# Attention with cached K and V on one core: x transposed on TensorE instead of by DMA, dummy products at the start, new order tables and load pacing

## The chip, the core and the metric

The kernel runs on one core of a Trainium2 chip. The core has a matrix engine (TensorE, in the profile PE, with its weight loads as PEld), three engines that work on rows of 128 partitions (VectorE, DVE; ScalarE, ACT; GpSimd, POOL), a queue engine that only issues transfers here (SyncE, SP), and 16 DMA engines that move data between the memory (HBM) and the on-chip memory (SBUF). TensorE writes into PSUM, which has eight banks of 128 partitions by 512 float32; the other engines read the banks and write SBUF. The metric is the time of one execution on the device in microseconds (us).

## What is computed

Two attention blocks, A and B, with the same shapes and their own inputs, written side by side into one output:

```python
B, Sq, D = 16, 64, 640
H, Sk, Dh = 32, 512, 128        # all arrays bfloat16

q = (x @ wq).reshape(B, Sq, H, Dh).transpose(0, 2, 1, 3)
scores = jnp.einsum("bhqd,bhkd->bhqk", q, k_cache) * (Dh ** -0.5)
p = softmax(scores, axis=-1)
o = jnp.einsum("bhqk,bhkd->bhqd", p, v_cache)
y = o.transpose(0, 2, 1, 3).reshape(B, Sq, H * Dh) @ wo
...
return jnp.concatenate([a, b], axis=-1)      # of blocks A and B
```

K and V of both blocks are 4 x 67 MB. All other inputs and the output are small beside them.

## The kernel before

**Tiles.** The batches are taken in pairs, so that the 64 queries of two batches fill 128 partitions; a pair and a head make a tile g. Two tiles (two heads of one pair) make a *step* m, two steps a *period* k. Sixteen heads of a pair make a group of four periods, and a pass is eight pairs with one half of the heads; there are four passes (block A heads 0 to 15, A 16 to 31, B, B), so 256 steps and 128 periods.

**One step.** K of two heads is loaded in rows and transposed by TensorE against an identity (KX, line 550: 32 products of 64 columns into two banks), copied to SBUF by VectorE (KE, 557). The scores of a tile are two products (SM, 596). VectorE takes the negated row maximum (MX, 605), ACT the exponential with the row sum (EX, 621), VectorE the reciprocal of two sums (RC2, 627), GpSimd multiplies (NM, 635). TensorE transposes the normalized P of a step, eight products into one bank (TR2, 644); the bank is copied to SBUF whole, for even steps by ACT (TA2, 656) and for odd steps by VectorE (TE2, 651). Then come the products with V (PV2, 666), one copy per period by ACT (OE4, 673), and the output projection, whose first 512 columns are done step by step (OP2, 681) and the other 128 once in a group (OX, 691). After an even pass ACT keeps the sums in `outp` (OVP and OXP, 699 and 704); after an odd one VectorE adds to them (OVF and OXF, 709 and 714) and ACT issues the store (ST, 720).

**Q.** The queries are made from x transposed (`xT_sb`, 128 rows of D by columns of queries). Sixteen heads of four pairs are needed at a time. The first of these are made in the first periods by QJ and QZ, the later ones, one per period, by QN (all line 567; five products over D); ACT copies them with the scale (QEJ, QEZ, QEN, 583). x of block A comes in by three DMA transposes (LDX, 751) of one, three and four pairs; x of block B comes later in plain rows (LDXR, 769), is transposed by TensorE (XT, 776: five products of 128 columns) and copied by ACT (XTE, 783).

**Order.** Nothing is scheduled on the chip. `build_plan` sorts each engine's list by a time in steps, which the tables `PHASES` give: for each kind of operation an offset in steps and a place within a period of `PERIOD` = 6.3. A table holds from a period on: here from 0, 16, 112 and from two before the end. Waits on semaphores follow from what each operation reads and writes. Banks: 0 sums, 1 the V products (and early Q), 2 to 5 scores (P^T uses 2 and 3, the 128 columns and x use 4), 6 and 7 K.

**Loads.** All loads are on SP's queue, in the order of a key: the step of first use less a lead (`LEAD` for K and V, `WLEAD` for weights). The planner also makes each load wait until TensorE has passed a position in its list, so that it is not issued far ahead:

```python
    for key, first, _, op in sorted(loads, key=lambda e: e[:3]):
        t_now = max(t_now, us(key))
        i = bisect.bisect_right(pe_us, min(t_now, us(first - cfg.BEFORE))) - 1
        if i >= 0:
            paced.append((op, progs["pe"][i]))
        progs["sp"].append(op)
        t_now += cfg.DMA_US[op.kind] * (op.aux[2] - op.aux[1] if op.kind == "LDX" else 1)
```

`us` turns steps into microseconds by the stretches of `STEP_US`; `t_now` starts at `START_US` and adds an assumed cost per load. So each load waits until TensorE has passed the place that stands for the earlier of two times: `t_now` (its key, or later where the loads ahead of it are assumed to take longer), and `BEFORE` steps ahead of its first use. Behind schedule, then, the second time binds. Nine K tiles (`NKB`) and five periods of V (`NVP`) fit on the chip.

## Time and profile before

| | us |
|---|---|
| median of three runs | 856.32 (855.03 to 856.79) |
| profiled execution | 857.66 |
| its span in the trace | 855.9 |
| TensorE busy | 805.9 (94%) |
| VectorE busy | 726.6 (85%) |
| ACT busy | 633.0 (74%) |
| GpSimd busy | 418.0 (49%) |
| moved by DMA | 297.13 MB, mean 347 GB/s |

How to read it: the page gives busy time by engine, then the span in 40 equal slices (each digit is the busy share in tenths; the last rows are the DMA engines' share and what they moved in GB/s). A busy share is an average over stages with different limits, so windows, waits and the timeline are read by stage. In a timeline or window line, xN is the number of instructions; what stands in brackets at the end is the engine's idle time before and what ended it. In the chain of work that ended last, each line is a start, a length and what ran or was waited for; a DMA line begins at its issue and ends with its landing. "SPq" is SP's queue itself. L numbers are lines of the kernel before.

### The profile page before, as it was taken

What the parts mean: (1) busy time and instruction counts of PE and PEld (TensorE: products, weight loads), DVE (VectorE), ACT (ScalarE), POOL (GpSimd) and SP (SyncE); (2) the same over time, 40 slices, a digit from 0 to 9 for tenths busy, and PEclk for the clock granted to TensorE, in tenths of its full rate; (3) what the DMA queues carried; (4) which work ended last, traced back from release to release, by engine and by line L of the source; (5) the groups of instructions that cost most, each with busy time, mean ns of one, the idle gap of its engine ahead of it and who ended that gap; (6) DMA issues with size and microseconds to landing.
All of it is one profiled execution on the core that took longest, in us unless ns stands there. A gap on an engine that the chain in (4) does not pass through costs nothing.

```text
span 855.9 us, 38296 instructions
## 1 busy us (share of the span) xinstructions
PE 805.9 (94%) x16953; PEld 561.8 (66%) x17084; DVE 726.6 (85%) x1184; ACT 633.0 (74%) x1450; POOL 418.0 (49%) x518
## 2 busy tenths in 40 slices
PE   5999999999999999999999899999999999999987
PEld 3566666666666766766666666666676666666665
DVE  3588888898888899898898788988888889889995
ACT  2677787787787777777777777777877867767775
POOL 0344554545544554554554445555455545446554
DMA  8999999999999999999999999999999999999993
GB/s 266 321 368 367 357 352 328 358 352 346 356 363 354 355 364 366 359 368 369 366 354 368 316 355 364 360 358 362 355 363 364 364 360 370 346 307 350 368 352 115
DMA packets 232581, 297.13 MB, mean 347 GB/s; under 512 B 14304, under 2 KB 166880, under 8 KB 232416
## 3 DMA queue, kind: packets, MB, share of 16 engines
q1 hardware_dynamic: 230112, 292.06, 100.2%
q8 instruction: 133, 2.18, 1.1%
q10 hardware_dynamic: 2304, 2.62, 0.9%
q14 instruction: 32, 0.26, 0.1%
HBM read 290.72 MB, written 2.62 MB: 343 GB/s over the span
## 4 chain that ended last, share of the span: by engine, by line
PE 81%; DMA 9%; DVE 3%; issue 3%; ACT 2%; POOL 1%; SPq 1%; POOLq 0%; ACTq 0%; DVEq 0%
PE ps L550 15%; PE ps L567 14%; PE ps L666 14%; PE ps L596 13%; PE ps L644 11%; PE ps L681 11%; DMA v_ring<-in_B_v_cache_dram 6%; PE ps L691 3%; DMA v_ring<-in_A_v_cache_dram 3%; DVE ktp_ring L557 2%; DVE negmax L605 1%; POOL pn_ring L635 1%; ACT p_ring L621 1%; DMA wq_sb<-in_A_wq_dram 1%; ACT pT_ring L656 1%
## 5 line engine op out<-in xcount | busy, mean ns | idle before, releaser
L635 POOL TENSOR_SCALAR pn_ring<-p_ring,recip 128x512 bf16<-128x512 bf16 x512 | 417.4, 846 | 429.9 <-DVE recip L627 403.2
L621 ACT ACTIVATE p_ring<-ps,negmax 128x512 bf16<-128x512 f32 x512 | 350.0, 689 | 77.5 <-DVE negmax L605 74.3
L557 DVE COPY ktp_ring<-ps 128x2048 bf16<-128x2048 bf16 x256 | 311.9, 1218 | 78.6 <-PE ps L550 78.3
L605 DVE TENSOR_REDUCE negmax<-ps 128x1 f32<-128x512 f32 x512 | 320.6, 683 | 19.7 <-PE ps L596 12.6
L550 PEld LDWEIGHTS ps<-ident,kn_ring 64*128 64x128 bf16 x8192 | 135.8, 95 | 99.2 <-issue 58.8
L550 PE MATMUL ps<-ident,kn_ring 64*128 64x64 bf16 x8192 | 167.4, 191 | 5.3 <-DVE ktp_ring L557 2.6
L673 ACT ACTIVATE oT_ring<-ps 128x512 bf16<-128x512 f32 x128 | 76.4, 597 | 123.7 <-PE ps L666 123.7
L567 PE MATMUL ps<-xT_sb,wq_sb 128*128 128x512 bf16 (+2 forms) x544 | 135.7, 376 | 26.8 <-issue 18.3
L666 PE MATMUL ps<-pT_ring,v_ring 128*128 128x64 bf16 x4096 | 142.7, 193 | 7.4 <-DMA v_ring<-in_B_v_cache_dram 4.1
L644 PEld LDWEIGHTS ps<-ident,pn_ring 128*128 128x128 bf16 x2048 | 124.9, 98 | 34.8 <-ACT p_ring L621 3.4
L644 PE MATMUL ps<-ident,pn_ring 128*128 128x128 bf16 x2048 | 137.4, 219 | 1.7 <-POOL pn_ring L635 1.2
L596 PE MATMUL ps<-ktp_ring,qc_ring 128*64 128x512 bf16 x1024 | 137.6, 387 | 1.2 <-issue 1.1
L666 PEld LDWEIGHTS ps<-pT_ring,v_ring 128*128 128x128 bf16 x4096 | 127.4, 98 | 15.9 <-DMA v_ring<-in_B_v_cache_dram 5.3
L681 PE MATMUL ps<-wo_sb,oT_ring 128*128 128x512 bf16 x497 | 132.1, 379 | 5.0 <-ACT pT_ring L656 2.5
L656 ACT ACTIVATE pT_ring<-ps 128x1024 bf16<-128x1024 bf16 x128 | 132.6, 1036 | 0.6 <-PE ps L644 0.4
L621 ACT ACTIVATION_READ_ACCUMULATOR p_ring<-ps,negmax 128x1 f32 x512 | 105.2, 206 | 0.0
L567 PEld LDWEIGHTS ps<-xT_sb,wq_sb 128*128 128x128 bf16 x660 | 54.9, 99 | 62.8 <-DMA wq_sb<-in_A_wq_dram 7.7
L651 DVE COPY pT_ring<-ps 128x1024 bf16<-128x1024 bf16 x128 | 86.3, 674 | 6.9 <-PE ps L644 6.8
L583 ACT ACTIVATE qc_ring<-ps 128x512 bf16<-128x512 f32 (+1 forms) x129 | 77.1, 597 | 14.2 <-PE ps L567 14.2
L596 PEld LDWEIGHTS ps<-ktp_ring,qc_ring 128*64 128x64 bf16 x1024 | 47.3, 109 | 37.4 <-issue 5.0
L681 PEld LDWEIGHTS ps<-wo_sb,oT_ring 128*128 128x128 bf16 x512 | 43.4, 98 | 31.8 <-ACT pT_ring L656 4.6
L627 DVE RECIPROCAL recip<-rowsum 128x2 f32<-128x2 f32 x256 | 39.9, 156 | 9.1 <-ACT p_ring L621 9.1
(16 smaller groups left out, 109.1 us busy)
## 6 DMA issues: line engine op xcount, KB each, us to landing
kn_ring<-in_A_k_cache_dram SPq DMA_DIRECT2D x128, 512.0 KB, 6.7
v_ring<-in_A_v_cache_dram SPq DMA_DIRECT2D x128, 512.0 KB, 6.6
kn_ring<-in_B_k_cache_dram SPq DMA_DIRECT2D x128, 512.0 KB, 6.4
v_ring<-in_B_v_cache_dram SPq DMA_DIRECT2D x128, 512.0 KB, 6.3
wq_sb<-in_A_wq_dram SPq DMA_DIRECT2D x8, 640.0 KB, 6.6
wo_sb<-in_A_wo_dram SPq DMA_DIRECT2D x8, 640.0 KB, 6.8
wq_sb<-in_B_wq_dram SPq DMA_DIRECT2D x8, 640.0 KB, 6.4
wo_sb<-in_B_wo_dram SPq DMA_DIRECT2D x8, 640.0 KB, 7.4
```

Source lines behind the costliest of these rows:

```text
L550: last = e.transpose(kt_ps[hs][:, 64 * t:64 * t + 64], kn_ring[r, m % NKB, t // 8, t % 8 * DH:(t % 8 + 1) * DH], ident[r, r])
L557: ins = e.tensor_copy(ktp_ring[:, ktslot(op.idx)], ps[:, b:b + 2, :].rearrange("p b s -> p (b s)").bitcast(BF16))
L567: last = e.matmul(dst[:, col:col + n], wq_sb[:, qslot(hh // G), kt, (hh % G) * DH:(hh % G + 1) * DH], xT_sb[:, kt, lo * 128:hi * 128], sta ...
L596: ins = e.matmul(s_bank(g)[64 * j:64 * j + 64, :], q[:, 64 * j:64 * j + 64], kt[:, sub, j], start=True, stop=True, tile_position=(0, 64 * j))
L605: ins = e.reduce_max(negmax[:, r:r + 1], s_bank(g), axis=AX.X, negate=True)
L621: ins = e.activation(p_ring[:, g % NP, :], s_bank(g), ACTF.Exp, bias=negmax[:, r:r + 1], scale=1.0, accum_out=rowsum[:, r:r + 1])
L635: ins = e.tensor_scalar(dst, src, recip[:, r:r + 1], 1.0, ALU.mult, ALU.mult)
L644: ins = e.transpose(pt_flat(m)[:, (4 * sub + t) * 128:(4 * sub + t + 1) * 128], pn_ring[:, g % NPN, t * 128:(t + 1) * 128], ident[:, :])
L651: ins = e.tensor_copy(pT_ring[:, m % NT].rearrange("p s t q -> p (s t q)"), pt_flat(m))
L656: ins = e.activation(pT_ring[:, m % NT].rearrange("p s t q -> p (s t q)"), pt_flat(m), ACTF.Copy)
L666: ins = e.matmul(qo_ps[:, col:col + 64], v_ring[:, m // 2 % NVP, j, 2 * (m % 2) + sub, t * DH:(t + 1) * DH], pT_ring[:, m % NT, sub, t, 64 ...
L681: ins = e.matmul(out_ps, oT_ring[:, m // 2 % NO, 2 * (m % 2) + sub, :], wo_sb[:, wslot(ps_, hh // G), hh % G, 0:N0], start=(hh == 0), stop ...
```

## The change

- x of block A no longer comes by DMA transposes. LDX becomes a plain load of rows into the (still unused) space of `outp`, and two new operations do the rest for each of the eight pairs: XI, five transposes on TensorE into bank 0, 1 or 4, and XIE, one copy of 128x640 by VectorE.
- WU: 32 products of 128 columns of the identity with ones into bank 5, first in TensorE's list, their result unused.
- K of step 1 goes through banks 4 and 5 instead of 6 and 7 (`kt_bank`).
- Order tables: the table from period 0 now holds for period 0 alone, with new ones from 1 and 3; those from 16, 112 and the last two are new as well. In the body TensorE's list stays the same but for OX, which moves between the two OP2; VectorE's KE 2 moves ahead of MX 1 1.
- P^T copies by head: from period 112 on the copy of an odd step is split. VectorE copies the first head's half (TE1), ACT the second's (TA1). Even steps stay whole on ACT. `pT` is tracked by half.
- Pacing: new `LEAD`, `WLEAD`, `STEP_US`, `START_US`, `BEFORE`, and a load whose position is the first one of TensorE's list now doesn't wait.
- MX2 and RC4, which no table used, are gone.

```diff
-    LEAD = 4.68
-    WLEAD = 4.56
-    STEP_US = ((8, 39.85), (32, 17.16), (256, 3.11))
-    DMA_US = dict(LDK=1.40, LDV=1.44, LDWQ=1.8, LDWO=1.8, LDX=1.3, LDXR=0.5)
-    START_US = -168.79
-    BEFORE = 1.75
+    LEAD = 5.37
+    WLEAD = 5.48
+    STEP_US = ((8, 3.68), (32, 27.17), (160, 3.12), (216, 3.1), (256, 3.43))
+    DMA_US = dict(LDK=1.40, LDV=1.44, LDWQ=1.8, LDWO=1.8, LDX=0.45, LDXR=0.5)
+    START_US = 210.96
+    BEFORE = 3.88
...
+    NWU = 32
...
+    def kt_bank(m):
+        return 4 if m == 1 else cfg.KTB[m % 2]
...
+        if kind in ("XI", "XIE"):
+            if k or sub >= NBP:
+                return None
+            b = (0, 1, 0, 1)[sub] if sub < QB else cfg.OXB
+            if kind == "XI":
+                return mk("pe", kind, sub, [("outp", sub, "V"), ("ident",)], [bank(b)], ts, aux=(b, sub))
+            return mk("dve", kind, sub, [], [bank(b), ("xT", sub)], ts, aux=(b, sub))
...
-        if kind in ("TE2", "TA2"):
-            return mk("dve" if kind == "TE2" else "act", kind, m, [], [bank(cfg.TRB[m % 2]), ("pT", m % cfg.NT)], ts)
+        if kind in ("TE2", "TA2", "TE1", "TA1"):
+            subs = (sub,) if kind[2] == "1" else (0, 1)
+            return mk("dve" if kind[1] == "E" else "act", kind, m, [],
+                      [bank(cfg.TRB[m % 2])] + [("pT", m % cfg.NT, i) for i in subs], ts, aux=subs)
...
+    progs["pe"] = [mk("pe", "WU", -1, [("ident",)], [], -99, aux=cfg.NWU)] + progs["pe"]
...
-        first = ("QN", 0, 0) if lo >= QB else ("QZ", 0, 0) if lo else ("QJ", 0, 0)
-        add([], first, cfg.WLEAD, -1, "LDX", (0, lo), [("xT", bp) for bp in range(lo, hi)], (0, lo, hi))
+        add([], ("XI", 0, lo), cfg.WLEAD, -1, "LDX", (0, lo), [("outp", bp, "V") for bp in range(lo, hi)], (0, lo, hi))
...
-        if i >= 0:
+        if i > 0:
             paced.append((op, progs["pe"][i]))
...
+        x_in = outp[:, :, :].bitcast(BF16)[:, :, 0:DN]
...
+        def pt_copy(m, subs):
+            c = slice(512 * subs[0], 512 * subs[-1] + 512)
+            return pT_ring[:, m % NT].rearrange("p s t q -> p (s t q)")[:, c], pt_flat(m)[:, c]
...
         def em_LDX(e, op):
             blk, lo, hi = op.aux
-            src = blocks[blk][0][2 * lo:2 * hi].rearrange("b q d -> (b q) d")
-            ins = e.dma_start_transpose(xT_sb[:, :, lo * 128:hi * 128], src)
+            src = blocks[blk][0][2 * lo:2 * hi].rearrange("(p b) q d -> (b q) p d", b=2)
+            ins = e.dma_start(x_in[:, lo:hi], src)
             return ins, ins
...
+        def em_XI(e, op):
+            b, bp = op.aux
+            first = last = None
+            for kt in range(KT):
+                last = e.transpose(ps[:, b, :].bitcast(BF16)[:, 128 * kt:128 * kt + 128],
+                                   x_in[:, bp, 128 * kt:128 * kt + 128], ident[:, :])
+                first = first or last
+            return first, last
+
+        def em_XIE(e, op):
+            b, bp = op.aux
+            ins = e.tensor_copy(xT_sb[:, :, bp * 128:bp * 128 + 128],
+                                ps[:, b, :].bitcast(BF16)[:, 0:D].rearrange("p (k q) -> p k q", k=KT))
+            return ins, ins
+
+        def em_WU(e, op):
+            first = last = None
+            for _ in range(op.aux):
+                last = e.matmul(ps[:, 5, 0:128], ident[:, :], ones_sb[:, :], start=True, stop=True)
+                first = first or last
+            return first, last
```

In the new first period TensorE's list runs WU, KX 0, XI 0, QJ, XI 1, KX 1, XI 2, XI 3, KX 3, then the first scores and QZ; SP's runs K0, x 0, wq 0, x 1 to 3, K1, K3 (which waits for XI 0), K2, wq 1 (which waits for QJ), x 4 to 7. ACT's copies six QZ results before the exponential of tile 0, which now comes fourth.

69 lines of the change are left out of this document (30 added, 39 removed), and 85 rows, old and new, of the table PHASES.

## The prediction

> **What bounds the kernel now.** I read the page first, then the windows, the timeline of the copy at L673 (one per period, so its start times are a clock of the run), the waits of TensorE and the chain. The page's second part shows two things full at once:
>
> ```profile
> PE   5999999999999999999999899999999999999987
> DVE  3588888898888899898898788988888889889995
> DMA  8999999999999999999999999999999999999993
> GB/s 266 321 368 367 357 352 328 358 352 346 356 363 354 355 364 366 359 368 369 366 354 368 316 355 364 360 358 362 355 363 364 364 360 370 346 307 350 368 352 115
> ```
>
> TensorE is busy nearly everywhere, and the DMA moves up to 370 GB/s but is often below it. Neither share says which one waits, so I go by stage. The start, in windows (PE, PEld, DVE, ACT, POOL, clock, DMA share, GB/s):
>
> ```profile
> 0.00:5.00 5.00, 0.00 (x0) 0.00 (x0) 0.00 (x0) 1.28 (x1) 0.69 (x6) 1.00 0.42 87
> 5.00:10.00 5.00, 2.30 (x24) 2.11 (x26) 0.00 (x0) 0.00 (x0) 0.00 (x0) 1.00 0.98 331
> 10.00:15.00 5.00, 2.35 (x79) 2.04 (x80) 2.45 (x2) 0.60 (x1) 0.00 (x0) 1.00 1.07 261
> 35.00:40.00 5.00, 4.55 (x86) 2.66 (x82) 3.42 (x7) 2.95 (x7) 1.62 (x2) 1.00 1.11 171
> ```
>
> TensorE does 4.65 us of work in the first 15 us, and the transfers sag at 10 to 15 and 35 to 40 us. The timeline shows why: L751 (the DMA transposes) holds SP's queue for 1.32, 6.55 and 8.29 us, against 0.5 to 0.6 for a plain load near it, and nothing is issued behind it meanwhile. The chain there, in order of time:
>
> ```profile
> 2.17 5.48 DMA wq_sb<-in_A_wq_dram
> ...
> 7.70 2.31 PE ps L567 x20
> ...
> 11.02 1.24 DVE ktp_ring L557
> ...
> 14.66 1.04 PE ps L550 x32
> ```
>
> From 10 to 15.7 us K transpose and K copy alternate in it, through one pair of banks, and 32 of L550 take 1.04 us where the chain has 0.57 for them from 19.10 us on. So TensorE runs slow at first, though the clock column says 1.00. In the body, L673 (timeline of ACT):
>
> ```profile
> 72.91 0.60 ACT L673 ACTIVATE oT_ring<-ps 128x512 bf16<-128x512 f32 x1 [0.80 <-PE ps L666]
> 79.03 0.60 ACT L673 ACTIVATE oT_ring<-ps 128x512 bf16<-128x512 f32 x1 [0.80 <-PE ps L666]
> ...
> 460.40 0.60 ACT L673 ACTIVATE oT_ring<-ps 128x512 bf16<-128x512 f32 x1 [0.69 <-PE ps L666]
> 467.74 0.60 ACT L673 ACTIVATE oT_ring<-ps 128x512 bf16<-128x512 f32 x1 [2.02 <-PE ps L666]
> ```
>
> An undisturbed period is 6.11 us (7.01 every fourth, with the 16 matmuls of L691; 6.39 with the transposes of L776). That is TensorE's own work back to back. Subtracting these from the 106 intervals between period 2 (52.80) and period 108 (737.90) leaves 10.8 us, in lumps of 0.1 to 1.2. The chain gives their cause:
>
> ```profile
> 458.78 7.77 DMA v_ring<-in_B_v_cache_dram
> 466.55 0.05 issue
> 466.60 0.65 PE ps L666 x16
> ```
>
> A V tile issued at 458.78 lands when it is wanted. It was held back on purpose: SP waits for TensorE's position (waits of SP: L761 and L764 on TensorE lines, over 500 us in all). Loads are late, the DMA is not out of rate.
>
> **The change, part by part.** One step is half a period, about 3.1 us.
>
> *Start.* Before, the first score product starts at 15.63 us and period 2 ends at 52.80. TensorE's work up to there, by warm rows of the chain, is 36.4 us: 11 K transposes at 0.57 us 6.3; QJ 1.15; 12 QZ at 1.09 and 4 at 0.85 (384 wide) 16.5; a QN 1.07; 16 SM at 0.245 3.9; 6 TR2 at 0.445 2.7; 6 PV2 at 0.52 3.1; 4 OP2 at 0.43 1.7. So 16.4 us are lost. After, the first score product needs K0, x 0 to 3, wq 0, K1 and K3: 2.88 MB. By the ramp seen before (2.09 MB by 10 us) that is 12.2 us; if plain loads run at 365 GB/s from 2.5 us, 10.4. With K3's transpose behind it I take 12. Four microseconds of work are then done, so 8 are lost. K1 gets banks of its own, so the copies and transposes of K0 and K1 no longer take turns. Cold clock: 14.66 to 18.7 us ran at about half rate, 2 us lost in that stretch; I charge 1.5 again, because TensorE has gaps until 12 us. Two go to hand-overs (TensorE stands idle 1.5 of the 30 us from 20 to 50 now, behind ACT lines of the chain). Lost: 11.5. Added: 40 transposes of x at L776's rate, 0.28 us per block (6.39 less 6.11), 2.24 us. Gain 16.4 - 11.5 - 2.2, say 2.7. Bounds: 5 if the loads ramp at once and the clock stays up, 0.5 if ACT, whose first-period order is new (head tile 0's EX behind six QEZ), holds up the first normalization. The eight XIE copies on VectorE lie between the 0.674 us of its 1024-wide copy and 0.40 (worked out for 512, from 1.218 for 2048 and 0.674 for 1024): 3 to 5.4 us, beside a VectorE busy 5.1 of 10 us in 20 to 30. New waits: SP holds K3, and wq 1 and x 4 to 7 behind it, until block 0 of x is transposed; by then 2.36 MB are issued, 6.4 us of transfer, so the engines do not starve. TensorE holds block 1 until ACT has copied QJ (0.60 us), with K1's transpose behind it, which waits for its load until later than that. The 32 dummies (0.11 us each, cold, as L567's first 20) run from about 1.4 to 5 us, when nothing has landed; they cost at most 0.6 to K0. Three transposes leave SP's queue, 16.2 us of it, and with them the sag at 35 to 40, worth 5 x (368-171)/368 = 2.7 us of transfer that nothing has to catch up later.
>
> [...]
>
> *Loads in the body.* The planner holds each load until TensorE passes its position, at latest BEFORE steps ahead of the use. Working both plans through, the V tiles of steps 34 to 220 are issued 3.5 steps ahead in the mean and 1.75 at least before (5.5 us, against page medians of 6.3 to 6.7 from issue to landing); after, 4.4 and 3.2 (10 us). K: 4.2 and 2.8 become 4.95 and 3.9. The lumps are 0.1 to 1.2 us, so 4 us more lead covers each. What is late next is the DMA's rate: a group of four periods moves 16 tiles of 0.524 MB and one weight slice of 0.655, 9.05 MB in 25.35 us, 357 GB/s, and up to 9.37 in 25.6 (366) where x of B and stores run too; full stretches gave 363 to 370. So lumps may survive there. Steps 6 to 20 go the other way, K 5.0 to 4.0 and V 4.4 to 3.6 steps, with landing medians of 8.8 and 9.7 us in the first 50 us; they may lose 1. Gain 7, bounds 0 and 10.8.
>
> *New orders.* TensorE's order in the body is the same but for L691, moved between two L681, and VectorE's swaps one K copy with one maximum: 0. At the change of tables three periods (109 to 111) run 6.84, 7.03 and 6.96 us with nothing landing late; the new table keeps the regular order there. Gain 1.2 of 2.5, bounds 0 and 2.5.
>
> *P^T by head*, from step 224, 16 times. There VectorE is the bound:
>
> ```profile
> 780.00:785.00 5.00, 4.84 (x120) 3.34 (x121) 4.98 (x10) 3.81 (x9) 2.93 (x4) 1.00 1.06 380
> ```
>
> Half of an odd copy leaves VectorE (0.674 - 0.40 = 0.27), and ACT gains one of about 0.6 (L673's 512), with a fourth of it free. Twelve periods bound by VectorE (many intervals of L673 are 5.49 there) give 3.3 at most; TensorE's own 4.92 (6.11 less 1.19 for the QN that is gone) is below that, but the DMA runs at 365 to 380 GB/s there, which caps the gain at the 2 us by which loads now start earlier. Gain 2, bounds 0 and 3.3. At the very end ACT copies 1.04 + 0.6 in a row, where VectorE's 0.67 lay beside: cost 0.2.
>
> *Sum:* 2.7 + 7 + 1.2 + 2 - 0.2 = 12.7. The profiled execution took 857.66 us (span 855.9), 1.3 above the median of 856.32. 857.7 - 12.7 = 845.0, and less 1.3 for the median 843.7: I say 843.5.
>
> **Rivals.**
> 1. *The DMA is the bound.* Earlier issue only lengthens the queue, as in 40 to 80 us, where landing takes 9 to 11 us at 368 GB/s. Then the 7 shrink to 1: 849.5. Against it: 338 to 340 GB/s between 120 and 160 us while loads were held. [...]
> 2. *The start gains nothing*: clock cold through the first period, or ACT late; 2.7 becomes -1.5: 847.5. For it: everything up to 31 us hangs on one chain.
> 3. *Slower: loads by turns.* With more in flight, an early K tile takes rate from the V tile that is due; landing rises from 6.5 to over 10 us, the new least lead. Each period then waits. At 0.12 us per period over 106 periods the gain is gone (12.7); at 0.3, 863. Against: at 40 to 80 us, with the queue full, only 0.9 us was lost in two periods.
> 4. *All lumps go and the start is quick*: 5 + 10 + 2 + 3: 837.
>
> **How the numbers follow.** Forecast (840 to 847) 0.55; rival 1 0.15; rival 2 0.12; rival 3 0.08; rival 4 0.10. The range 836 to 851 takes in all but rival 3 and what lies outside the bounds. A measurement of this kernel tells about 0.2% (1.7 us) from no change: faster 0.89, same 0.03, slower 0.08.
>
> **What would show it.** Right: first score product at 11 to 13 us; period 2 at 49 to 51; no sag at 35 to 40; body intervals at 6.11 and 7.01, TensorE's waits for V near nothing; periods 109 to 111 below 6.5; VectorE below 95% after 780 us. Wrong: landing times near 10 us with V waits kept (rivals 1 and 3), L550 still at 1.04 us after 19 us (rival 2).

## The result, and the profile after

The changed kernel takes 850.32 us (median; 845.12 to 853.53), the kernel before 856.20 in the same comparison: a ratio of 0.9936, 95% interval 0.9912 to 0.9959. It is faster, as forecast, but by 5.9 us, less than half of the 12.7 of the sum. The profiled execution took 852.97 us, with a span of 851.0. In what follows L numbers are lines of the changed kernel (the P^T copy per period that served as a clock, L673 before, is L701; VectorE's K copy, L557 before, is L593).

The page's second part, the span in 40 slices:

```profile
PE   8999999999999999999999998999999999999996
GB/s 306 360 354 349 369 354 352 348 338 362 354 352 353 369 369 363 359 360 367 364 362 367 364 360 349 321 362 362 360 360 363 366 369 365 366 339 352 370 321 89
```

The start is fuller (306 GB/s in the first slice, 266 before; TensorE 8, before 5); the middle looks as it did. The same windows as before (PE, PEld, DVE, ACT, POOL, granted clock, DMA share, GB/s):

```profile
0.00:5.00 5.00, 3.59 (x36) 3.40 (x38) 0.00 (x0) 1.28 (x1) 0.68 (x6) 1.00 0.63 178
5.00:10.00 5.00, 3.03 (x58) 2.37 (x57) 1.62 (x2) 0.44 (x1) 0.00 (x0) 0.99 0.99 338
10.00:15.00 5.00, 4.79 (x88) 3.52 (x90) 2.87 (x5) 0.16 (x1) 0.00 (x0) 0.67 0.91 309
35.00:40.00 5.00, 4.67 (x60) 2.50 (x59) 3.86 (x7) 3.42 (x8) 1.61 (x2) 1.00 1.07 362
```

The two sags of the start are gone or smaller (309 and 362 GB/s, before 261 and 171), and TensorE does more in the first 15 us. But the clock column of 10 to 15 us reads 0.67. VectorE from 780 to 830 us, after and then before:

```profile
780.00:830.00 50.00, 46.41 (x1103) 34.03 (x1109) 47.41 (x83) 41.99 (x96) 27.61 (x34) 1.00 1.02 344
780.00:830.00 50.00, 46.55 (x1095) 33.64 (x1104) 48.88 (x82) 37.39 (x86) 26.93 (x34) 1.00 1.06 368
```

It is a little less full (47.41 of 50 us, before 48.88), and ACT is fuller (41.99, before 37.39).

TensorE's waits between 50 and 735 us (us in total, times, longest):

```profile
PE ps L603 <- issue: 16.9, 106, 0.2
PE ps L694 <- issue: 1.9, 3, 1.1
...
```

No wait for a load is left; before, the V product waited for V loads for 5.8 us there. (The first line is no loss: in most periods the record of the first of the five QN products is missing, x543 in the group on the page against x660 in other runs of the same work, and its place looks like a wait.) What is left are stretches in which TensorE waits for no semaphore and does nothing. The chain shows two of them, in order of time (start, length, what):

```profile
516.18 0.77 PE ps L632 x6
516.95 0.73 issue
517.68 0.41 PE ps L632 x2
...
529.18 0.69 PE ps L694 x20
529.87 1.06 issue
530.92 0.51 PE ps L694 x12
```

Both lie in the middle of a row of like products that all have what they need. Last, the change of tables, by the timeline of L701:

```profile
740.97 0.60 ACT L701 ACTIVATE oT_ring<-ps 128x512 bf16<-128x512 f32 x1 [0.66 <-PE ps L694]
747.08 0.60 ACT L701 ACTIVATE oT_ring<-ps 128x512 bf16<-128x512 f32 x1 [0.80 <-PE ps L694]
753.19 0.60 ACT L701 ACTIVATE oT_ring<-ps 128x512 bf16<-128x512 f32 x1 [0.38 <-PE ps L694]
760.20 0.60 ACT L701 ACTIVATE oT_ring<-ps 128x512 bf16<-128x512 f32 x1 [0.27 <-PE ps L694]
```

The intervals are 6.11, 6.11 and 7.01, where before they were 7.03, 6.96 and 7.01: the periods 109 to 111 are regular (the first of them, which ends at 740.97, took 6.24, before 6.84).

From the start times of this copy the span falls into stages. The table gives them for every kernel below (one profiled execution each, us), with V waits of TensorE between 50 and 735 us and the sum of the pauses over 0.25 us that lie inside a row of like products and wait for no semaphore (from 50 us to the end; a pause is the distance from one product's start to the next beyond the usual one, and the sums move by about 0.5 us with what one takes as usual). From period 127 to the end it is 5.13 to 5.16 everywhere.

| kernel | median, ratio to before | to period 2 | 2 to 108 | 108 to 112 | 112 to 124 | 124 to 127 | V waits | pauses |
|---|---|---|---|---|---|---|---|---|
| before | - | 52.80 | 685.10 | 27.84 | 71.03 | 13.96 | 5.8 | 5.5 |
| after | 850.32, 0.9936 | 51.24 | 683.48 | 25.48 | 70.18 | 15.43 | 0 | 6.5 |
| after, again | 850.08, 0.9923 | 51.27 | 679.07 | 25.48 | 71.10 | 15.45 | 0 | 5.7 |
| before, new pacing only | 856.51, 0.9998 | 53.16 | 682.64 | 27.84 | 71.59 | 13.94 | 2.0 | 8.5 |
| after, old pacing | 859.20, 1.0016 | 54.64 | 689.59 | 25.48 | 69.70 | 15.44 | 5.9 | 3.4 |
| before, few V loads | 844.11, 0.9848 | 52.77 | 675.55 | 27.20 | 67.88 | 13.72 | 0.9 | 0 |
| after, few V loads | 840.56, 0.9818 | 52.33 | 674.54 | 25.35 | 67.38 | 14.16 | 0 | 0 |
| after, half the V loads | 840.87, 0.9814 | 50.45 | 674.70 | 25.35 | 67.71 | 14.36 | 0 | 0 |
| TE2 ahead of OXF | 852.50, 0.9945 | 51.95 | 679.12 | 25.35 | 70.43 | 15.45 | 0 | 5.7 |
| V named first | 848.99, 0.9918 | 50.61 | 684.70 | 25.93 | 69.19 | 14.15 | 0.2 | 9.8 |
| odd P^T copy whole | 852.21, 0.9948 | 53.54 | 679.56 | 25.48 | 71.75 | 15.64 | 0 | 5.6 |
| old table from 112 | 854.01, 0.9979 | 52.04 | 679.75 | 25.83 | 73.07 | 15.05 | 0 | 4.1 |
| old last table | 851.53, 0.9929 | 52.58 | 682.07 | 25.48 | 73.82 | 14.63 | 0.5 | 7.4 |
| no dummies | 851.56, 0.9946 | 52.44 | 679.90 | 25.48 | 70.02 | 15.44 | 0 | 4.2 |
| two dummies more | 849.06, 0.9917 | 49.79 | 680.75 | 25.48 | 71.53 | 15.43 | 0 | 6.8 |
| three mends | 847.97, 0.9897 | 50.54 | 679.01 | 25.35 | 70.09 | 14.71 | 0 | 5.4 |
| all mends | 846.95, 0.9890 | 50.30 | 681.98 | 26.25 | 69.92 | 14.15 | 2.4 | 7.2 |

Against before, with the mean of the two profiles of after: start 1.5, body 3.8, periods 108 to 124 2.8, last periods -1.5; 6.6 in all, and the medians give 5.9. So the body gave about half of its 7, the transition more than its 1.2, the late periods next to nothing of their 2, and the end took back seven times its 0.2.

### The profile page after: what moved, and what is told of

It is laid out like the page before. It is cut to its first block, busy times and chain, and to the rows that moved or that the text cites. A ratio compares the mean times of both kernels' runs of the same rounds, so it can differ in the third digit from the quotient of the medians.

```text
span 851.0 us, 38366 instructions
## 1 busy us (share of the span) xinstructions
PE 811.3 (95%) x17025; PEld 566.4 (67%) x17156; DVE 727.9 (86%) x1192; ACT 644.7 (76%) x1466; POOL 417.1 (49%) x518
## 3 DMA queue, kind: packets, MB, share of 16 engines
q1 hardware_dynamic: 225968, 292.06, 100.3%
## 4 chain that ended last, share of the span: by engine, by line
PE 89%; issue 3%; ACT 3%; DMA 2%; DVE 2%; SPq 0%; ACTq 0%
PE ps L586 17%; PE ps L694 15%; PE ps L603 15%; PE ps L632 14%; PE ps L670 13%; PE ps L709 12%; PE ps L719 3%; ACT p_ring L647 2%; DMA v_ring<-in_A_v_cache_dram 1%; DVE negmax L641 1%; ACT pT_ring L684 1%; DMA wq_sb<-in_A_wq_dram 1%; DVE ktp_ring L593 1%; PE ps L804 0%; PE ps L813 0%
## 5 line engine op out<-in xcount | busy, mean ns | idle before, releaser
L647 ACT ACTIVATE p_ring<-ps,negmax 128x512 bf16<-128x512 f32 x512 | 349.0, 688 | 74.0 <-DVE negmax L641 68.5
L593 DVE COPY ktp_ring<-ps 128x2048 bf16<-128x2048 bf16 x256 | 312.1, 1219 | 56.3 <-PE ps L586 56.2
L641 DVE TENSOR_REDUCE negmax<-ps 128x1 f32<-128x512 f32 x512 | 328.3, 683 | 16.2 <-PE ps L632 8.5
L586 PEld LDWEIGHTS ps<-ident,kn_ring 64*128 64x128 bf16 x8192 | 136.8, 95 | 107.9 <-issue 96.4
L586 PE MATMUL ps<-ident,kn_ring 64*128 64x64 bf16 x8192 | 169.2, 191 | 3.3 <-issue 1.4
L603 PE MATMUL ps<-xT_sb,wq_sb 128*128 128x512 bf16 (+2 forms) x543 | 133.4, 372 | 19.0 <-issue 18.1
L694 PE MATMUL ps<-pT_ring,v_ring 128*128 128x64 bf16 x4096 | 143.5, 194 | 2.8 <-issue 1.9
L701 ACT ACTIVATE oT_ring<-ps 128x512 bf16<-128x512 f32 x128 | 76.4, 597 | 91.7 <-PE ps L694 91.7
L684 ACT ACTIVATE pT_ring<-ps 128x1024 bf16<-128x1024 bf16 (+1 forms) x144 | 140.9, 987 | 3.0 <-DVE pT_ring L680 2.2
L709 PE MATMUL ps<-wo_sb,oT_ring 128*128 128x512 bf16 x498 | 135.3, 379 | 4.0 <-issue 1.9
L632 PE MATMUL ps<-ktp_ring,qc_ring 128*64 128x512 bf16 x1024 | 135.5, 385 | 0.7 <-issue 0.7
L694 PEld LDWEIGHTS ps<-pT_ring,v_ring 128*128 128x128 bf16 x4096 | 128.2, 98 | 9.6 <-issue 2.4
L647 ACT ACTIVATION_READ_ACCUMULATOR p_ring<-ps,negmax 128x1 f32 x512 | 104.8, 205 | 0.0
L680 DVE COPY pT_ring<-ps 128x1024 bf16<-128x1024 bf16 (+1 forms) x128 | 82.5, 644 | 14.6 <-PE ps L670 14.1
L603 PEld LDWEIGHTS ps<-xT_sb,wq_sb 128*128 128x128 bf16 x660 | 53.8, 98 | 54.0 <-issue 1.1
L632 PEld LDWEIGHTS ps<-ktp_ring,qc_ring 128*64 128x64 bf16 x1024 | 47.2, 109 | 34.1 <-issue 1.3
```

The lines of the kernel that those rows point to most:

```text
L586: last = e.transpose(kt_ps[hs][:, 64 * t:64 * t + 64], kn_ring[r, m % NKB, t // 8, t % 8 * DH:(t % 8 + 1) * DH], ident[r, r])
L593: ins = e.tensor_copy(ktp_ring[:, ktslot(op.idx)], ps[:, b:b + 2, :].rearrange("p b s -> p (b s)").bitcast(BF16))
L603: last = e.matmul(dst[:, col:col + n], wq_sb[:, qslot(hh // G), kt, (hh % G) * DH:(hh % G + 1) * DH], xT_sb[:, kt, lo * 128:hi * 128], sta ...
L632: ins = e.matmul(s_bank(g)[64 * j:64 * j + 64, :], q[:, 64 * j:64 * j + 64], kt[:, sub, j], start=True, stop=True, tile_position=(0, 64 * j))
L641: ins = e.reduce_max(negmax[:, r:r + 1], s_bank(g), axis=AX.X, negate=True)
L647: ins = e.activation(p_ring[:, g % NP, :], s_bank(g), ACTF.Exp, bias=negmax[:, r:r + 1], scale=1.0, accum_out=rowsum[:, r:r + 1])
```

## Experiments

**The same kernel again.** Kernel after, unchanged.

> The changed kernel again, beside the next three, so that they can be compared with it on the same chip. Both theories: 0.9936 of the kernel before, 0.991 to 0.996. From its first profile: 22 body intervals of the copy at L701 that are 0.1 to 0.16 us over 6.11, and 5.49 us per period after step 226.

850.08 us, ratio 0.9923 (0.9897 to 0.995). Its executions lie between 844.8 and 857.0. The table's two rows of after agree within 0.03 us in start, transition and end, and differ by 4.4 us in the body: a single profile of the body is one draw, and medians and lines must decide.

**The pacing alone**, on the kernel before.

```diff
-    LEAD = 4.68
-    WLEAD = 4.56
-    STEP_US = ((8, 39.85), (32, 17.16), (256, 3.11))
+    LEAD = 5.37
+    WLEAD = 5.48
+    STEP_US = ((8, 3.68), (32, 27.17), (160, 3.12), (216, 3.1), (256, 3.43))
-    START_US = -168.79
-    BEFORE = 1.75
+    START_US = 210.96
+    BEFORE = 3.88
```

> The kernel before, with only the pacing numbers of the changed one (LEAD, WLEAD, STEP_US, START_US, BEFORE). Theory of the prediction (V tiles issued at the last moment cost the body 7 to 10.8 us): 848 to 850, TensorE's waits for V gone. Theory now: the waits for V go, but only some 5 us of the 10.8 were theirs, the rest are stalls of TensorE 1.2 to 1.6 us behind the arrival of a 16 KB instruction packet, and these stay: 850 to 853, body excess of 4 to 6 us. Rival (loads by turns): waits for V stay and the time is 856 or more.

856.51 us, ratio 0.9998 (0.9983 to 1.0013): nothing, give or take 1.3 us. V waits fell from 5.8 to 2.0 us (1.4 of them in period 3, to which the new numbers issue V later), but this profile has 8.5 us of pauses without a semaphore. The reading that removing a V wait removes its time seemed to fall here.

**The old pacing, in the changed kernel**: the same five numbers back.

> After, with the earlier five pacing numbers. Theory A (V waits and instruction fetch stalls are two faces of one full DMA, and the pacing trades one for the other): V waits of 4 to 6 us come back to TensorE's list between 50 and 735 us, the stalls without semaphore shrink, and the time stays within 1.5 us of after: 849 to 852. Theory B (the forecast's: each V wait costs its full time): 5 to 7 us slower, 855 to 857.

859.20 us, ratio 1.0016 (0.9997 to 1.0034): 9 us slower than after, more than the whole gain. Its waits of TensorE from 50 to 735 us:

```profile
PE ps L694 <- DMA v_ring<-in_B_v_cache_dram: 3.8, 6, 1.3
PE ps L694 <- issue: 3.3, 6, 1.2
PE ps L694 <- DMA v_ring<-in_A_v_cache_dram: 2.1, 4, 0.9
```

The V waits are back at 5.9 us, the stages show 6 to 10.5 us more in the body and 3.4 more at the start (with the old numbers SP holds loads back between 5 and 10 us: 136 GB/s there, 338 after). The pauses without a semaphore are 2.7 us in this stage, inside the 1.7 to 4.8 of the two profiles of after. Theory B, that a V wait costs its time, stands for the changed kernel. The trade of theory A does not show in the body; but 3.4 us of pauses over the whole span is the least of the fourteen profiles with all loads, so one profile does not rule out a small one. Why the same numbers gave nothing in the kernel before stays open: its start could not gain, since the DMA transposes held SP there (16.2 us in all, by the timeline of before), and for its body I have one profile (2.5 us shorter), too few against the spread seen above.

**No V loads.** After, with V loads issued for the first ten periods only.

```diff
+        if k < 2 * cfg.NVP:
             add([("PV2", 2 * (k - cfg.NVP) + 1, 0)] if k >= cfg.NVP else [], ("PV2", 2 * k, 0), cfg.LEAD - j, 2, "LDV", m,
                 [("v", k % cfg.NVP, j)], m)
```

> The changed kernel, without the loads of V after the first ten periods: the V products go on with tiles that stay in place, so half of the transferred bytes are left out (and most of the output is of the wrong V). Theory (what is left of the body's excess is TensorE's own instruction fetch, which is late because it shares the DMA engines with full load queues): the stalls behind instruction packets go, body from period 2 to 108 at 674 to 677 us against 679 to 683, the 0.13 us of the VectorE order stay, and the periods after 113 stay at 5.49, since a loop through ACT bounds them. Rival (fetch stalls come from the code's own place, not from the DMA load): they stay at 3 to 6 us in sum. Rival for the end (the DMA bounds the last stretch): intervals fall towards 5.1.

840.56 us. Every pause without a semaphore is gone, the body is 674.54 against a floor of 674.33 (106 times 6.113, and what the stores' groups and x of B add), and the late periods run at 5.38 instead of 5.49. So leaving out V loads is worth about 10 us, though no load was waited for. About 6 of them are the pauses (6.5 and 5.7 us in the two profiles of after). About 3.5 need no full queue: 1.2 in the body, about 1 in the late periods and 1.3 at the end (14.16 after 15.43) come from the place of a wait, which the missing loads change as well. "V named first" below gets these back with all loads in place, and takes up the miss in this expectation.

**Half the V loads.** The condition is `k < 2 * cfg.NVP or k % 2 == 0`.

> After, with V loads of every second period only, from the eleventh on (result not the reference's): about 280 GB/s in place of 350. Theory A (the instruction packets are late only when the queues in front of them are full): the stalls without semaphore vanish as they do with no V loads at all, 840 to 842.5 us. Theory C (they grow with the load): about half stays, 844.5 to 846 us.

840.87 us: as good as none. TensorE's list of waits from 50 to 735 us is empty. The page's DMA queue lines (packets, MB, share of 16 engines' span), of this run first:

```profile
q1 hardware_dynamic: 163664, 230.19, 83.9%
```

and of after:

```profile
q1 hardware_dynamic: 225968, 292.06, 100.3%
q8 instruction: 134, 2.20, 1.1%
```

With the load queue at 84% there is no pause, at 100% there are some 6 us of them. The pauses do not grow with the load, they come with the full queue: theory A (where between 84% and 100% they begin, no run shows). What is late then seems to be in the second queue. Its 134 packets of 16 KB seem, by their number, to bring the instructions of TensorE: one comes every 6.2 us, and 255 of TensorE's instructions (products and weight loads) run in that time; on the page no other engine has more than 1466 instructions in the whole span. In the trace's packet records of after, packets end at 516.27 and 529.54 us; the two pauses shown above end at 517.68 and 530.92, 1.4 us later. In the fourteen profiles with full loads there are 147 such pauses over 0.25 us, and every one ends 1.16 to 1.75 us after the end of such a packet; by chance about one in ten would. That the pause is a wait for the packet, and that the packet came late, is inferred from this: the trace does not show when it was asked for.

**No V loads, before.** The same edit in the kernel before.

> Before, with V loads issued for the first ten periods only (the later P V products read what lies in the buffers, so the result is not the reference's). Theory A (both kernels lose the same 9 to 10 us to the full DMA, the changed one in other places): 846 to 848 us, so that the same leaving out is worth as much as in after (9.5 us) and the 6 us between the kernels are orders and start alone. Theory B (the forecast's: before loses 10.8 us in its body to V waits and the pacing takes most of that away, after has other losses): 843 to 845 us, 12 us or more under before.

844.11 us, 12.8 less than before in the same comparison. Theory B was right on the size, but not on its cause: of the 12.8 us, 5.8 less the 0.9 left are V waits and 5.5 pauses. Without V loads the two kernels differ by 3.5 us, and that is start, orders and transition. The other 2.4 of the 5.9 appear only with the loads, and the parts fit: the changed kernel has none of the 4.9 us of V waits that go here, has as many pauses as before (6.5 and 5.7 us against 5.5), and loses about 2.2 more to the place of a wait (1.2 in the body and 1.0 more at the end; the late periods fall from 5.49 to 5.38 or less in both kernels). It also shows how steady a kernel is without the fetch pauses: its executions lie within 0.5 us of each other, those of before within 6.

**VectorE's order in the body.** In both profiles of after the same nine body intervals (41, 45, 49, 53, 57, 61, 65, 101 and 105, each the first of a group of four periods, in passes whose groups end with a store) are 6.23 to 6.25 instead of 6.11, 1.2 us in all. VectorE, timeline of after at one of them:

```profile
295.25 0.29 DVE L742 TENSOR_TENSOR out_sb<-ps,outp 128x128 bf16<-128x128 f32 x1 [1.01 <-PE ps L719]
295.46 0.68 DVE L680 COPY pT_ring<-ps 128x1024 bf16<-128x1024 bf16 x1
...
296.65 1.21 DVE L593 COPY ktp_ring<-ps 128x2048 bf16<-128x2048 bf16 x1
```

and before, at the same place:

```profile
296.68 0.67 DVE L651 COPY pT_ring<-ps 128x1024 bf16<-128x1024 bf16 x1
298.20 0.29 DVE L714 TENSOR_TENSOR out_sb<-ps,outp 128x128 bf16<-128x128 f32 x1 [0.85 <-PE ps L691]
...
299.01 1.22 DVE L557 COPY ktp_ring<-ps 128x2048 bf16<-128x2048 bf16 x1
```

Before, the P^T copy was done when VectorE stood waiting 0.85 us for the 128-column sums. After, the output sum of 128 columns stands in front of it, VectorE waits 1.01 us with the P^T copy behind, and both it and the K copy come later: the K copy starts 0.57 us ahead of that period's L701, before 0.73. The experiment puts it back:

```diff
-          ("KE", 2, 0, 2.61), ("MX", 1, 1, 3.18), ("RC2", 0, 0, 3.78), ("OXF", -3, 0, 4.23), ("TE2", -1, 0, 4.74),
+          ("KE", 2, 0, 2.61), ("MX", 1, 1, 3.18), ("RC2", 0, 0, 3.78), ("TE2", -1, 0, 4.22), ("OXF", -3, 0, 4.74),
```

> The changed kernel, with VectorE's whole copy of P^T (TE2) put ahead of OXF again in the table from period 16, and nothing else. Theory (new VectorE order): VectorE waits in order for the 16 matmuls of OX, with TE2 now behind that wait; K's copy then starts 0.16 us late relative to the period, the exponentials and ACT's copy of P^T with it, and TensorE waits 0.13 us once in each group. So the 22 intervals of 6.24 fall back to 6.11 and the time falls by 2.6 us (1.5 to 3.5) against the changed kernel. Rival (the 0.13 come from fuller transfer queues or from the longer lead): they stay, and the time is the same within 1 us.

852.50 us, ratio 0.9945 (0.992 to 0.9969): no gain in the total. In its profile eight of the nine intervals are back at 6.11 and one (65) is left. The sum expected had counted every interval between 6.2 and 6.3 as of this kind; only these nine are, the others (eight in one profile of after, three in the other) mostly change their places from profile to profile. So the mechanism is shown, and its worth, 1.1 us, is below what the medians resolve.

**V named first.** The 0.13 us has a second cause. The V product waits for two things, V and the P^T copy of ACT. Where an operation of TensorE has two waits, the kernel's own planner (`prune_waits`, the same in both kernels) moves one of them to the last instruction of the operation ahead:

```python
                if (eng == "pe" and len(keep) > 1 and pc[eng] and prog[pc[eng] - 1].early is None):
                    before = prog[pc[eng] - 1]
                    for w in keep:
                        if snap[w].get(before.sem, 0) < before.count:
                            before.early = w
                            break
```

It takes the first of them that it can, in the order in which the inputs are named. In after that is the P^T wait, and it stands on the last K-transpose product, so TensorE waits for the copy one product too early. It is the program that puts the wait there. Without V loads the V product has one wait and carries it itself, which is why those intervals vanished there although I expected them to stay.

```diff
-            return mk("pe", "PV2", m, [("pT", m % cfg.NT, 0), ("pT", m % cfg.NT, 1), ("v", k % cfg.NVP, 0), ("v", k % cfg.NVP, 1)], [bank(1)], ts)
+            return mk("pe", "PV2", m, [("v", k % cfg.NVP, 0), ("v", k % cfg.NVP, 1), ("pT", m % cfg.NT, 0), ("pT", m % cfg.NT, 1)], [bank(1)], ts)
```

> After, with one list turned round: the second P V product names V ahead of P^T, so that the V wait, not the wait for ScalarE's P^T copy, is the one that is put on the last K-transpose product in front of it. Theory (the 0.13 us of the intervals behind the stores' groups, and 0.11 us of each period after 112, come from the P^T wait standing one instruction too early): the 22 intervals of 6.24 us in the loop fall to 6.11 or nearly (-2 to -2.6 us between periods 2 and 108), the intervals after 112 from 5.49 to about 5.38 (-1.2 to -1.5 us over 112 to 124), in all 846 to 848 us and a ratio of about 0.99. Rival (the waits only change names: V's now holds the last K-transpose product, or instruction fetches swamp it): the intervals stay at 6.24 and 5.49, within 1.5 us of the 850 of after.

848.99 us, ratio 0.9918 (0.9894 to 0.9942), a little outside what was expected. Both signs came as the theory has them: of the nine intervals one is left (57), and the late periods go to 5.38. L701 in after:

```profile
789.75 0.60 ACT L701 ACTIVATE oT_ring<-ps 128x512 bf16<-128x512 f32 x1
795.24 0.60 ACT L701 ACTIVATE oT_ring<-ps 128x512 bf16<-128x512 f32 x1 [0.15 <-PE ps L694]
```

and here:

```profile
795.80 0.60 ACT L701 ACTIVATE oT_ring<-ps 128x512 bf16<-128x512 f32 x1
801.18 0.60 ACT L701 ACTIVATE oT_ring<-ps 128x512 bf16<-128x512 f32 x1
```

5.49 became 5.38, as in all late periods without a pause or a group's end. The last periods gain as well (14.15 against 15.43). But this profile has 9.8 us of fetch pauses, the most of all, and its body is the second longest: the pauses' own spread is larger than what the edit saves.

**The odd P^T copy whole again**, on VectorE.

```diff
-          ("EX", 1, 0, 3.03), ("OVP", -99, 0, 3.42), ("TA2", -2, 0, 3.96), ("TA1", -1, 1, 4.2), ("EX", 1, 1, 5.66)),
+          ("EX", 1, 0, 3.03), ("OVP", -99, 0, 3.42), ("TA2", -2, 0, 3.96), ("EX", 1, 1, 5.66)),
...
-          ("KE", 2, 0, 3.61), ("RC2", 0, 0, 3.87), ("OVF", -3, 0, 3.89), ("TE1", -1, 0, 3.93), ("MX", 1, 1, 4.88),
+          ("KE", 2, 0, 3.61), ("RC2", 0, 0, 3.87), ("OVF", -3, 0, 3.89), ("TE2", -1, 0, 3.93), ("MX", 1, 1, 4.88),
```

(and the same two in the last table)

> The changed kernel, with the odd P^T copies after step 224 whole on VectorE again, and nothing else. Theory of the prediction (VectorE bounds that stretch, the split relieves it by 0.27 us in 12 periods): 3 us slower, the intervals go from 5.49 to about 5.76 or the stretch from period 112 to 124 grows by 3. Rival (a second loop of the same length bounds it: scores, maximum, three exponentials, ACT's P^T copy, V products, scores, which the split doesn't shorten): intervals stay at 5.49, the time is within 1.5 us of the changed kernel, and the last three periods may even be shorter, since ACT loses 16 copies of 0.6 us.

852.21 us, ratio 0.9948 (0.9924 to 0.9973). 112 to 124 takes 71.75, after 70.18 and 71.10: the split is worth about 1 us at most, with pauses in this stage that make 1 us uncertain. The quiet intervals are 5.50 to 5.55, after 5.49: the rival's sign. The 2.3 us more up to period 2 are a later landing of the first weights in this profile (9.30 us, after 7.37), not the edit. The end stays at 15.64: the split is not what made it longer.

**The old table from 112.** The whole table of the kernel before for the periods 112 to 125.

```diff
-         (("SM", 0, 0, 0.0), ("SM", 0, 1, 0.21), ("SM", 1, 0, 0.43), ("SM", 1, 1, 0.64), ("KX", 2, 0, 0.79),
-           ("OP2", -4, 0, 2.67), ("TR2", -2, 0, 2.98), ("OP2", -3, 0, 3.28), ("TR2", -1, 0, 3.46),
...
+         (("SM", 0, 0, 0.0), ("SM", 0, 1, 0.21), ("SM", 1, 0, 0.43), ("SM", 1, 1, 0.64), ("KX", 2, 0, 0.75),
+           ("OP2", -4, 0, 0.84), ("TR2", -2, 0, 3.32), ("TR2", -1, 0, 3.58), ("OP2", -3, 0, 4.07),
...
```

> The changed kernel with the kernel before's table from period 112 to 125 (P^T whole there). Theory: the 2.36 us between the copies of periods 108 and 112 (27.84 before, 25.48 after) come from that table alone: back to 27.8, and 112 to 124 at 71 to 71.7; total 2.4 to 3.5 us more than the changed kernel, 852 to 854. Rival (they come from the body's table or the pacing): 25.5 stays.

854.01 us, ratio 0.9979 (0.9961 to 0.9997): most of the gain is gone. The loss is not where I looked for it: 108 to 112 takes 25.83, nearly as in after, and 112 to 124 takes 73.07. Together 98.90, where before has 98.87 and after 95.66 and 96.58. So the three slow periods of before were no fault of the join of two tables alone; with the body's new table in front, the same loss comes a few periods later. The new table from 112, with the split in it, is worth 2.3 to 3.2 us over both stages.

**The old table for the last two periods.**

```diff
-         (("SM", 0, 0, 0.0), ("SM", 0, 1, 0.21), ("SM", 1, 0, 0.43), ("OX", -69, 0, 0.46), ("SM", 1, 1, 0.64),
-           ("TR2", -2, 0, 2.47), ("KX", 2, 0, 2.48), ("TR2", -1, 0, 2.67), ("OP2", -4, 0, 3.17), ("OP2", -3, 0, 4.16),
...
-           ("TE1", -1, 0, 5.68)),
+         (("SM", 0, 0, 0.0), ("SM", 0, 1, 0.21), ("SM", 1, 0, 0.43), ("SM", 1, 1, 0.64), ("KX", 2, 0, 0.75),
+           ("TR2", -2, 0, 2.9), ("OX", -53, 0, 3.05), ("TR2", -1, 0, 3.05), ("OP2", -4, 0, 5.23), ("KX", 5, 0, 5.31),
...
+           ("TE2", -1, 0, 5.49)),
```

> The changed kernel with the kernel before's table for the last two periods (so P^T of these two is copied whole). Theory: that table costs the 1.5 us between the copies of periods 124 and 127 (15.4 against 13.96 before; 15.6 with whole P^T copies, so it is the order and not the split): 13.8 to 14.2, total 1.5 us less than the changed kernel. Rival (the loss comes in from the periods before, over the later V or K tiles): 15.4 stays.

851.53 us, ratio 0.9929 (0.9907 to 0.9952): not to be told from after by its total. 124 to 127 takes 14.63 instead of 15.43; the copies of the periods 125 and 126 come 6.24 and 5.09 us apart (after 6.26 and 6.24, before 5.33 and 5.31). The old table gives back about half of the 1.5 us that the end lost. Naming V first gives back 1.3 without it (above, 14.15) and no more with it (below, 14.15 again): what the new last table lost, it lost for the most part to the misplaced P^T wait.

**No dummies.**

```diff
-    progs["pe"] = [mk("pe", "WU", -1, [("ident",)], [], -99, aux=cfg.NWU)] + progs["pe"]
```

> The changed kernel without the 32 dummy products at the start. The clock rows of three profiles say that the dummies raise the clock 5 to 6.5 us after the start for one window of 3.4 us, that it falls again for one or two windows, and is up for good from 13.3 to 16.9. Theory A (the dummies warm the clock too early to help): clock up for good at the same place, QJ's 20 products take 2.3 instead of 1.3 to 2.3 us, period 2 ends within 1 us of 51.3. Theory B (they are worth most of the start's gain): clock up after 18 us, period 2 ends 1.5 us or more later. In both the total is 850 to 852.

851.56 us, ratio 0.9946 (0.993 to 0.9963). Period 2 ends at 52.44, after at 51.24, but the first weight slice landed at 8.19 here and at 7.37 in after: from that landing to period 2 it is 44.25 us, exactly as in the repeat of after (landing 7.02, period 2 at 51.27), where the dummies stand; in the first profile of after it is 43.87, and in that of V named first, whose start is the same, 43.01. So they are worth between nothing and 1.2 us where they stand, and the clock goes with it: it is up for good from 13.29 us in the first profile of after and from 13.69 with V named first, but from 15.22 in the repeat and from 15.69 here. The chain of after:

```profile
1.77 5.60 DMA wq_sb<-in_A_wq_dram
7.42 0.24 PE ps L813
...
8.23 1.30 PE ps L603 x20
...
10.21 0.71 PE ps L813 x5
10.92 0.97 PE ps L586 x32
11.89 1.18 PE ps L813 x10
13.07 0.68 PE ps L586 x32
```

32 of L586 take 0.97 us at 10.92 and 0.57 later in the kernel. The clock rows of the trace have full speed from 6.46 us for 3.41 us, half for the next 3.41, and full from 13.29 on. The dummies end at 5 us; from 6.46 to 9.88 us TensorE is busy for 1.57 of 3.41 us, and at 9.88 the clock falls to half. The chain also shows another loss: the planner has put the wait for the weight slice on the last x transpose (L813 at 7.42), so the copy of x behind it and QJ (L603) come late, QJ 0.86 us after the landing.

**Two dummies more, just ahead of QJ.**

```diff
+    at_qj = [o.kind for o in progs["pe"]].index("QJ")
+    progs["pe"].insert(at_qj, mk("pe", "WU", -2, [("ident",)], [], progs["pe"][at_qj].ts - 0.01, aux=2))
```

> The changed kernel with two more dummy products between XI 0 and QJ, so that the wait for wq 0 no longer sits on the last product of XI 0 (an operation's second wait is put on the last instruction of the one before it). Theory: XI 0 and its copy are done 1 us before wq 0 lands, QJ starts 0.05 us after the landing and not 0.85, SP issues K3 1 us earlier, the first scores and period 2 come 0.7 to 1 us earlier against the same landing. Rival: the first scores wait for K1 or x 1 to 3 anyway, period 2 is the same within 0.3 us.

849.06 us, ratio 0.9917 (0.9885 to 0.9949). The first score product comes at 11.95, in after at 13.68, and period 2 ends at 49.79, 1.5 earlier. From the landing of the first weights (7.27) that is 42.52 us, against 43.87 and 44.25 in after and 43.01 with V named first: 0.5 to 1.7 us less. The weight wait now sits on a dummy; the clock rows have full speed from 4.49 us on without a break. In its chain:

```profile
8.73 0.24 PE ps L605
...
10.11 0.57 PE ps L588 x32
```

The 32 K transposes take 0.57 us at 10.11. What holds QJ next is x of the other pairs, which lands at 8.69: the next x transposes need it, and the planner has put their wait on the last product of QJ. Of the gain, wait and clock are not separated.

**Three mends together**: P^T copy ahead of the output sum, the old last table, and twenty dummies ahead of QJ instead of two.

> The changed kernel with TE2 ahead of OXF in the body, the kernel before's last table, and 20 more dummy products between XI 0 and QJ, which keep TensorE busy while wq 0 is awaited. Sum of the three as the theories have them: 1.8 (profile of the first), 1.5 and 1 to 2 us, so 845.5 to 847 against 850.1. Rival (fetch stalls move with the code's place and swamp it): within 1.5 us of the changed kernel.

847.97 us, ratio 0.9897 (0.9875 to 0.992): between what the theory and what the rival gives. The signs came: from the landing of the first weights (9.06) to period 2 it is 41.48 us, of the nine intervals one is left in part (6.15), and the end takes 14.71.

**All mends**: the same with V named first, and eight dummies more behind QJ.

> The kernel of the best time so far (848.0 us: second transpose copy ahead of the output copy in the last-but-one body table, the earlier last-periods table, twenty dummy products in front of the first Q product), with V named first in the second P V product and eight more dummy products behind the Q product of the first period. Theory: what the three parts gave adds to the 0.11 us of each late period (-1.2 to -1.5 us): 844 to 846.5 us, under the 848.0 in the same direction as the run with V first alone; the last stretch stays at 14.7 us, the stretch 112 to 124 falls below 69. Rival (late periods stay at 5.49, fetch stalls decide): 847 to 849 us.

846.95 us, ratio 0.9890 (0.9868 to 0.9912), the lowest median of the study, but not to be told from the three mends (0.9897); it is 2.0 us below the kernel with V first alone, where the intervals of the ratios also overlap. It is 0.5 us above the expected stretch. Of the signs, the quiet late periods came (5.38); the end, expected at 14.7, is 14.15; 112 to 124 stayed at 69.92, with 3.7 us of fetch pauses after 735 us. A new wait took 2.4 us in period 3, in its chain:

```profile
47.78 9.89 DMA v_ring<-in_A_v_cache_dram
```

The start became faster than V of period 3 can be there.

## Why the prediction was right or wrong

**Direction, range: right.** 850.3 lies inside 836 to 851, but near its upper end; the forecast stretch of 840 to 847 was missed. Rival 1 gave 849.5. Its premise is shown in one part: a full DMA queue costs the changed kernel about 6 us (the pauses, which are there with the load queue at 100.3% and gone at 83.9%). Its form is not: no load is waited for. That the time lies near rival 1's, and inside the range, is partly luck: the transition gained 1.2 us more than was booked, and every other part less. (Rival 3 is mis-added: 0.3 us in each of 106 periods on top of 843.5 gives 875, not 863.) The mean rate between 60 and 735 us is 359 GB/s, before 358; but 300 to 340 us ran at 367, so in these runs the mean is not a ceiling.

**Start, 2.7: size off, 1.5 measured.** The sags went as worked out. The first score product came at 13.68, not 12: QJ started 0.86 us late behind a wait placed on the x transpose, and the clock was at half from 9.88 to 13.29. The charge of 1.5 for a cold clock was about right in kind, but I gave nothing for the dummies' place; two more ahead of QJ bring the first score product to 11.95 and 0.5 to 1.7 us back at period 2. (The trace of before has no clock rows at all, so the 1.00 in its clock column says nothing; the same kernel with the new pacing has rows, full speed from 18.38 us on.) The new start is mostly transposes, and the clock came up in the midst of them: it rose to full at 13.29 after 3.41 us in which TensorE did transposes alone, for 3.08 us (the chain above from 10.21), and without dummies it rose at 15.69 after 3.41 us of nothing else.

**Loads in the body, 7: 3.8 measured, and this is the step that failed most.** That the V waits go was right (5.8 to 0, and 5.9 again with the old pacing). Wrong was "The lumps are 0.1 to 1.2 us, so 4 us more lead covers each": of the 10.8 us of lumps only 5.8 were V waits. The list of TensorE's waits between 50 and 735 us in the kernel before had said so:

```profile
PE ps L666 <- DMA v_ring<-in_B_v_cache_dram: 4.1, 7, 1.2
PE ps L666 <- DMA v_ring<-in_A_v_cache_dram: 1.7, 3, 1.2
PE ps L666 <- issue: 0.8, 2, 0.6
PE ps L550 <- issue: 0.6, 3, 0.2
```

There are 1.4 us on "issue" beside the V waits, and the chain had "issue" inside rows of like products; I took all lumps for one cause after seeing it in one of them. Of the rest, 2.3 us are pauses inside rows, which end behind instruction packets; more lead does not cover them, and they stayed (4.8 and 1.7 us in the two profiles of after). The other 2.7 were not told apart. With few V loads all but 1.2 of the 10.8 goes (675.55 against the floor of 674.33). So the step could give 5.8 and not 7, and the 3.8 of the stage is about that, less the 1.2 of the next paragraph and about 1 us more of pauses. One run stays against it: in the kernel before, the new pacing took 3.8 us of V waits away and left the median where it was.

**New orders: "VectorE's swaps one K copy with one maximum: 0" failed.** The output sum also moved ahead of the P^T copy (and TensorE's transposes of the later x behind a K transpose), and what I did not ask is what stands behind a waiting instruction on VectorE. It costs 0.13 us in nine periods, 1.2 us. The transition was right and larger: 108 to 112 gained 2.4 against 1.2.

**P^T by head, 2: about nothing in the stage 112 to 124** (0.85 and -0.07), of which the old table shows that it would be worse by 2 to 3 without the new one. "Twelve periods bound by VectorE, 3.3 at most" failed: VectorE did fall a little (48.88 to 47.41 of 50 us), and the quiet interval stayed at 5.49 to the hundredth, because another loop has almost the same length. The chain of after has it (L694 is the V product, L632 the scores, L641 the maximum, L647 the exponential, L684 ACT's P^T copy, L586 the K transpose):

```profile
817.81 1.04 PE ps L694 x32
818.85 0.35 PE ps L632 x2
...
819.22 0.70 DVE negmax L641
...
821.26 0.87 ACT p_ring L647 x3
822.12 0.92 ACT pT_ring L684
...
823.09 0.20 PE ps L586
823.29 1.04 PE ps L694 x32
```

It runs V product, score, maximum, exponentials, ACT's copy of 0.92, the end of a K transpose, V product, in 5.48 us; 0.11 us of it is the misplaced P^T wait, so by itself it takes 5.38. VectorE's own loop is no longer than that: before, with few V loads and the odd copy whole, has quiet late periods of 5.36 to 5.38. It was checkable beforehand: the relieved engine gives back only the distance to the next loop. The DMA cap that I put at 2 is not what binds (5.38 with fewer loads and with full ones).

**The end, -0.2: -1.5 measured.** I priced one copy and not the new last table, whose periods 125 and 126 take 6.26 and 6.24 instead of 5.33 and 5.31, nor the place of the P^T wait, without which 1.3 of the 1.5 come back.

The named signs: period 2 at 49 to 51 (51.24, just off), no sag at 35 to 40 (362 GB/s), V waits near nothing, periods 109 to 111 below 6.5 (6.24, 6.11, 6.11), VectorE below 95% after 780 us (94.8% up to 830, so just): right. First score product (13.68) and body intervals at 6.11 throughout: wrong. The two signs against, landing near 10 us with V waits kept and L550's slow rate after 19 us, did not appear.

## What to carry to other kernels

Sum the lumps of a stage by what ended each of them before giving one cause the whole; time on "issue" inside a row of like instructions may be instruction fetch: here each such pause ended 1.16 to 1.75 us after a packet of the instruction queue, and there was none with the load queue at 84% or less. When an order table changes, ask of every instruction that may wait what has come to stand behind it, and when an engine is relieved, measure the next loop before booking the gain. Look where your planner puts a second wait: here it sits on the operation ahead, and the order in which the inputs are named decides which one. When an experiment leaves loads out, it leaves their waits out too, so see what else moves with them. Try dummy products for the clock right in front of the first real work too: here the 32 at the very start were worth between nothing and 1.2 us, and two more ahead of QJ 0.5 to 1.7, the moved wait included.

## What the runs showed of the hardware

- TensorE pauses inside rows of like products that wait for nothing, each ending 1.16 to 1.75 us after a 16 KB instruction packet (about 1.08 us each): 3.4 to 9.8 us per execution in the fourteen profiles with the load queue at 99.7% or more of the engines' time, none in the three at 84%, 64% and 63%. Executions of after differ by 8 to 12 us, those without such pauses by 0.5 to 3.3.
- The clock rows of after change at 6.46, 9.88 and 13.29 us: full speed for 3.41 us, with TensorE busy for 1.57 of them; half for the next 3.41, with TensorE busy for 3.08, on transposes alone; then full. In after with few V loads TensorE was busy for 2.96 us from 10.32 to 13.73, at half clock, and the clock stayed at half; in all mends it was busy for 1.77 us from 53.57 to 56.98, at full clock, and the clock stayed full. These are single stretches of single profiles; what the clock follows was not tested beyond them.
